# The first block of a convolution feeding a two-layer network: one part of the tokens convolved on TensorE, another in 256 columns, and the last sums made elsewhere

## The chip, the core and the metric

The kernel runs on one core of a Trainium2 chip (trn2). The metric is the device time of one execution in microseconds, as the median of several executions. A core has TensorE (PE, matrix multiplication; PEld is its weight load), VectorE (DVE), ScalarE (ACT), GpSimd (POOL) and SyncE (SP, here only the queue that issues most DMAs).

## The reference, cut to what matters

```python
# weight (8 heads, 7 taps); x (8, 4096, 192); w_in (192, 2048); w_out (2048, 192)
w = softmax(weight, axis=-1)
x_pad = concatenate([zeros((B, 6, D)), x], axis=1)
y[b, s, h, g] = sum over k of w[h, k] * x_pad[b, s + k, h, g]     # a causal filter of 7 taps
h = y.reshape(32768, 192) @ w_in
g = where(h >= 1, h, where(h <= -1, 0, (h + 1) ** 2 / 4))
out = g @ w_out
```

## The kernel before

**Tiles and steps.** The 32768 tokens are cut into 64 blocks of 512 (TB). The 2048 hidden units are cut into 8 pairs of 128. A step q is one block s and one pair j (q = 8 s + j). In step q TensorE does mm1(q), the first layer into the PSUM tile h, and then the second layer of step q - 2 (mm2, or mm2_first for the first two blocks). The tile h has two buffers (pool ps_h), so mm1(q + 2) waits until step q has read its h for the last time. That last read is most(q) in the first eight steps and act_max(q) later.

**Channels.** The 192 channels are 128 and 64. A pair of blocks c (tokens A and tokens B) is convolved in three units: "a" holds channels 0 to 127 of tokens A, "b" the same of tokens B, and "r" holds channels 128 to 191 of both, tokens A on partitions 0 to 63 (TOP) and tokens B on 64 to 127 (BOT). A unit is loaded (raw), transposed to channels on partitions (xT), and its seven taps are summed into y. Blocks from the second on need y split into a high and a low part (split, split_rest), and each part also with its two halves of partitions exchanged. The exchange is DMAs from SBUF to SBUF (swapped), two for each part, issued by SP.

**The first block** (s = 0, steps 0 to 7) has a program of its own. Its activation of step q is a ScalarE pass (Relu, then Square) and most(q) on VectorE. The weights arrive as 64-bit numbers in chunks 0 to 9 (words) and are turned into floats on the chip: ScalarE makes m and r (floats), VectorE makes wa in two instructions and adds r (bits), which gives WI (first layer, chunk j needed by mm1(j)) and WF (second layer). Chunk n's slot in words is free again when floats(n) is done, and chunk n + 3 is loaded into it.

**Convolution of the first two blocks before the change.** Unit a: taps 4, 5, 6 on VectorE, taps 0 to 3 and the join of the two on TensorE (taps_pe). Unit r: all seven taps on VectorE for both token blocks at once, then a TensorE copy of the upper half (both_pe). Only then do VectorE's bits of chunks 0 and 1 follow, and mm1(0). Unit b: taps on VectorE in steps 1 to 5 (FIRST_B), split in step 6. split_rest of unit r is in step 5. mm1(8) is the first matmul group of tokens B: it reads the high and low parts of b, of b exchanged, and of r.

**Order.** The order on every engine is the order in which the code is written (manual_schedule), and each engine works its list strictly in that order. Semaphores join the engines. DMAs of one queue are issued in order.

**The end** (evac_last): the last block's sums stand in two PSUM halves for each of accr (channels 128 up) and accm. ScalarE copies half 0 to SBUF; VectorE copies the first 256 columns of half 1 and adds the two halves in the other 256. TensorE transposes each block of 128 tokens, summing the halves as it does, and each of four results is copied and stored.

Of the kernel before, what the change touches and what calls it, by code (L numbers as in the profile page):

```python
# [8 lines left out]
F32 = mybir.dt.float32  # L9
# [21 lines left out]
def lightconv_then_ffn(ctx: ExitStack, tc: tile.TileContext, x, weight, w_in, w_out, out):  # L31
# [52 lines left out]
    def load_raw(t0s, chans, engs=None):  # L84


        raw = xin.tile([P, NG, SQ], F32, name="raw")
        first = [t0 % S == 0 for t0 in t0s]
        for i0 in (0, 2):
            if first[i0]:  # L90
                nc.gpsimd.memset(raw[i0 * SQ:(i0 + 2) * SQ, 0, :], 0.0)
        for i in range(4):
            lo = 1 if first[i] else 0
            src = xf[t0s[i] - SQ + lo * SQ:t0s[i] + TB, chans[i]:chans[i] + SQ]
            (engs[i] if engs else nc.sync).dma_start(
                out=raw[i * SQ:(i + 1) * SQ, lo:, :],
                in_=src.rearrange("(j a) b -> a j b", a=SQ),
            )
        return raw

    def load_plain(eng, c0, n, *t0s):

        raw = xin.tile([P, NG, SQ], F32, name="raw").rearrange("p j b -> p (j b)")[:, 0:TB]
        to = raw.rearrange("p (t i c) -> p t i c", t=TB // P, i=len(t0s))
        for i, t0 in enumerate(t0s):
            eng.dma_start(out=to[:, :, i], in_=xf[t0:t0 + TB, c0:c0 + n].rearrange(
                "(t p) c -> p t c", p=P))
        return raw

    def load_unit(c, u, engs=None):  # L110
        ta, tb = 2 * c * TB, (2 * c + 1) * TB
        if u == "r":
# [8 lines left out]
    class Conv:  # L121


        def __init__(self, c, u, raw):
            self.c, self.u, self.raw = c, u, raw
            self.wsel = 1 if u == "r" else 0

        def transpose(self):
            self.xT = xw.tile([P, NG * SQ], F32, name="xT")
            self.y = xw.tile([P, TB], F32, name="y")  # L130
            nc.vector.transpose(out=self.xT, in_=self.raw.rearrange("p j b -> p (j b)"))

        def transpose_pe(self, ps):

            self.ps = ps
            for t in range(0, TB, P):
                nc.tensor.transpose(ps[:, t:t + P], self.raw[:, t:t + P], one)  # L137

        def tail_pe(self, c0, ps):

            nc.tensor.matmul(ps, self.raw[:, c0:c0 + P], one[:, P - K + 1:], start=True, stop=True)

        def room(self):

            self.xT = xw.tile([P, NG * SQ], F32, name="xT")
            self.y = xw.tile([P, TB], F32, name="y")
            nc.vector.memset(self.xT[:, SH:SQ], 0.0)

        def fetch(self):
            nc.scalar.copy(self.xT[:, SQ:], self.ps)  # L150

        def taps_pe(self, banks, ks):

# [34 lines left out]
        def taps(self, *ks):  # L188
            y = self.y
            for k in ks:  # L190
                tap, wt = self.xT[:, SH + k:SH + k + TB], wk[:, self.wsel, k:k + 1]
                if k == 0:
                    nc.scalar.mul(y, tap, wt)
                else:
                    p = xw.tile([P, TB], F32, name="p", bufs=3)
                    nc.scalar.mul(p, tap, wt)  # L196
                    nc.gpsimd.tensor_add(y, y, p)  # L197
# [20 lines left out]
        def both_pe(self, bank):  # L218

            self.ys = [ps_o.tile([P, TB], F32, name=bank)]  # L220
            nc.tensor.matmul(self.ys[0], ident[TOP], self.y[TOP], start=True, stop=True)

        def split_rest(self):
# [253 lines left out]
    def evac_last(s):  # L477

# [5 lines left out]
        for a in "rm":  # L484
            u, v = part[a] = [ob.tile([P, TB], F32, name="t", bufs=4) for _ in range(2)]
# [4 lines left out]
        ps = [ps_h.tile([P, 2, TB], F32, name="h") for _ in range(2)]  # L490
        y = [ob.tile([P, TB], F32, name="sum") for _ in range(2)]
        for b in range(TB // P):
            i, e, n = b // 2, b % 2, slice(b * P, (b + 1) * P)
            for a, i_n, c in (("r", ident[:, 0:DR], slice(P, D)), ("m", plain, slice(0, P))):
                ts = part[a][i:]
                for t in ts:
                    nc.tensor.matmul(ps[e][:, i, c], t[:, n], i_n, start=(t is ts[0]),  # L497
                                     stop=(t is ts[-1]))
            to = y[i][:, e * D:(e + 1) * D]
            if e == 0:  # L500
                nc.scalar.copy(to, ps[e][:, i, 0:D])
# [33 lines left out]
    idle_matmuls(6)  # L535
    nc.scalar.dma_start(out=heads, in_=weight)
    raw_a = load_plain(nc.sync, 0, P, 0)
    raw_r = load_plain(nc.sync, P, DR, 0, TB)
    chunks[0].load(nc.sync)
    for n in range(1, 5):  # L540
        if n == 3:
            raw_b = load_unit(0, "b")
# [5 lines left out]
    for sel, c0, reps in ((0, 0, 1), (1, P, 2)):  # L548
# [22 lines left out]
    conv_a.fetch()  # L571
# [37 lines left out]
    whole(2, 0, CI)  # L609
    floats(2, CI)  # L610
# [8 lines left out]
    FIRST_B = {1: (0, 1), 2: (2,), 3: (3, 4), 4: (5,), 5: (6,)}  # L619
# [24 lines left out]
    for j in range(NPAIR):  # L644
        PARTS[5 + j].append((j, False))
# [127 lines left out]
```

## Time and profile before

| | us |
|---|---|
| median of 3 runs | 2262.39 (2261.7 to 2262.97) |
| the profiled execution | 2263.13 |
| its span, first to last instruction | 2261.3 |
| TensorE busy | 2253.2 |
| VectorE, ScalarE, GpSimd busy | 2110.2, 1694.2, 1160.5 |

The profiled execution is 0.74 us above the median. Of its 2263.13 us, 1.8 lie outside the span. All times in the tables below are counted from the span's first instruction.

### The profile page before, as it was taken

Reading aid. Unit: us, or ns where it says so; the run is one execution under the profiler, and the core shown is the slowest. Engines: PE = TensorE matmul, PEld = TensorE weight load, DVE = VectorE, ACT = ScalarE, POOL = GpSimd, SP = SyncE. Lnnn points to the kernel's source line nnn. Section 1 sums busy time; section 2 is a strip of 40 time slices with the busy share of each in tenths; the row PEclk is TensorE's granted clock in tenths of the full one; section 3 lists DMA queues with packets and bytes.
Section 4 is the critical chain, followed back from the end, with each engine's and each line's share of the span. In section 5 each row is a group of like instructions: output and inputs, shape, how many; then the busy total and the mean of one; then the engine's idle time right before and its main releaser. Section 6 shows DMA issues by size and latency. Waiting matters only on the chain.

```text
span 2261.3 us, 48195 instructions
## 1 busy us (share of the span) xinstructions
PE 2253.2 (100%) x19676; PEld 2096.3 (93%) x19676; DVE 2110.2 (93%) x1862; ACT 1694.2 (75%) x2141; POOL 1160.5 (51%) x846
## 2 busy tenths in 40 slices
PE   9999999999999999999999999999999999999999
PEld 6999999999999999999999999999999999999998
DVE  8899999999999999999999999999999999999997
ACT  6678777778777777777877777877777777787775
POOL 0446544466445565455654446644556545565451
PEclk9999999999999999999999999999999999999999
DMA  7221222222222222222122222222222222212211
GB/s 160 49 51 36 48 49 49 51 47 42 46 46 51 53 39 51 49 46 53 36 49 48 49 51 48 42 46 46 50 53 39 51 49 46 54 36 49 48 34 24
DMA packets 441852, 110.94 MB, mean 49 GB/s; under 512 B 410144, under 2 KB 417312, under 8 KB 441632
## 3 DMA queue, kind: packets, MB, share of 16 engines
q1 hardware_dynamic: 441472, 107.77, 25.8%
q8 instruction: 155, 2.54, 0.5%
q14 instruction: 65, 0.53, 0.1%
q10 hardware_dynamic: 160, 0.10, 0.0%
HBM read 32.83 MB, written 25.17 MB: 26 GB/s over the span
## 4 chain that ended last, share of the span: by engine, by line
PE 99%; DVE 0%; ACT 0%; issue 0%; POOL 0%; POOLq 0%; DVEq 0%
PE h L351 47%; PE accm L395 30%; PE accr L395 20%; PE accm L373 1%; PE accr L373 1%; DVE y L185 0%; PE h L497 0%; PE accm L529 0%; DVE g L679 0%; ACT g L669 0%; DVE y L183 0%; PE h L137 0%; PE accr L578 0%; DVE gh L311 0%; DVE wa L306 0%
## 5 line engine op out<-in xcount | busy, mean ns | idle before, releaser
L197 POOL TENSOR_TENSOR y<-y,p 128x512 f32<-128x512 f32 x558 | 779.9, 1398 | 794.2 <-DVE g L417 559.8
L430 DVE TENSOR_TENSOR gl<-g,gh 128x1024 fp32r<-128x1024 f32 (+1 forms) x497 | 734.0, 1477 | 27.2 <-ACT gh L424 22.7
L412 ACT ACTIVATE g<-g 128x1024 f32<-128x1024 f32 (+1 forms) x505 | 535.3, 1060 | 242.9 <-DVE g L406 234.2
L424 ACT CAST gh<-g 128x1024 fp32r<-128x1024 f32 (+1 forms) x497 | 521.6, 1050 | 239.4 <-DVE g L417 229.1
L406 DVE TENSOR_SCALAR g<-h 128x1024 f32<-128x1024 f32 (+1 forms) x505 | 610.0, 1208 | 94.7 <-PE h L351 86.4
L351 PE MATMUL h<-hi,w 64*128 64x512 f32 x4032 | 653.6, 389 | 0.0
L417 DVE TENSOR_TENSOR g<-h,g 128x1024 f32<-128x1024 f32 (+1 forms) x505 | 613.8, 1216 | 9.8 <-ACT g L412 2.4
L395 PE MATMUL accm<-gh,w 64*128 64x512 f32 x3968 | 548.1, 388 | 0.0
L351 PEld LDWEIGHTS h<-hi,w 64*128 64x128 f32 x4032 | 431.6, 184 | 29.1
L395 PEld LDWEIGHTS accm<-gh,w 64*128 64x128 f32 x3968 | 425.1, 184 | 28.9
L351 PE MATMUL h<-lo,w 64*128 64x512 f32 x2016 | 421.4, 388 | 0.0
L196 ACT ACTIVATE p<-xT,wk 128x512 f32<-128x512 f32 x558 | 372.1, 709 | 0.2 <-POOL y L197 0.2
L395 PE MATMUL accr<-gl,wr 64*128 64x512 f32 x1984 | 321.0, 388 | 0.0
L395 PE MATMUL accr<-gh,wr 64*128 64x512 f32 x1984 | 321.0, 388 | 0.0
L395 PE MATMUL accm<-gl,w 64*128 64x512 f32 x1984 | 321.0, 388 | 0.0
L351 PE MATMUL h<-rhi,w 64*128 64x512 f32 x1008 | 310.9, 388 | 0.0
L351 PE MATMUL h<-rh,w 64*128 64x512 f32 x1008 | 310.9, 388 | 0.0
L351 PEld LDWEIGHTS h<-lo,w 64*128 64x128 f32 x2016 | 216.0, 184 | 14.7
L443 POOL TENSOR_TENSOR sum<-t 128x512 f32<-128x512 f32 (+1 forms) x126 | 162.8, 1313 | 128.5 <-ACT t L442 128.5
L395 PEld LDWEIGHTS accr<-gl,wr 64*128 64x128 f32 x1984 | 212.6, 184 | 14.6 <-DVE gl L430 0.2
L395 PEld LDWEIGHTS accm<-gl,w 64*128 64x128 f32 x1984 | 212.6, 184 | 14.5
L395 PEld LDWEIGHTS accr<-gh,wr 64*128 64x128 f32 x1984 | 212.6, 184 | 14.5
(114 smaller groups left out, 1939.9 us busy)
## 6 DMA issues: line engine op xcount, KB each, us to landing
out_dram<-osb SPq DMA_DIRECT2D x366, 64.0 KB, 2.0
raw<-in_x_dram SPq DMA_DIRECT2D x334, 68.0 KB, 2.4
hi<-hi SPq DMA_DIRECT2D x126, 128.0 KB, 2.4
lo<-lo SPq DMA_DIRECT2D x126, 128.0 KB, 2.3
rhi<-rh SPq DMA_DIRECT2D x64, 128.0 KB, 2.3
rlo<-rl SPq DMA_DIRECT2D x64, 128.0 KB, 2.4
words<-in_moe_w_in_dram SPq DMA_DIRECT2D x16, 192.0 KB, 4.2
words<-in_moe_w_out_dram SPq DMA_DIRECT2D x8, 384.0 KB, 4.2
```

Source lines behind the costliest of these rows:

```text
L196: nc.scalar.mul(p, tap, wt)
L197: nc.gpsimd.tensor_add(y, y, p)
L351: nc.tensor.matmul(h[:, e, :], w[HALVES[e], COL[u][e]:COL[u][e] + P], x[e], start=(n == 0), stop=(n == len(mms) - 1))
L373: nc.tensor.matmul(accs[s][a, i][:, c0:c0 + D], g[half, e, b * P:(b + 1) * P], w[half, e, :], start=False, stop=(j == NPAIR - 1 and e == 1 ...
L395: nc.tensor.matmul(accs[s][a, i], st, g[HALVES[i], e, :], start=(j == 0 and n == first[a]), stop=(j == NPAIR - 1 and n == last[a]))
L406: nc.vector.tensor_scalar(out=g[:, e, :], in0=hs[q][:, e, :], scalar1=-1.0, scalar2=1.0, op0=ALU.max, op1=ALU.min)
L412: nc.scalar.activation(g[:, e, :], g[:, e, :], AF.Square, bias=0.5, scale=0.5)
L417: nc.vector.tensor_tensor(out=g[:, e, :], in0=h[:, e, :], in1=g[:, e, :], op=ALU.max)
L424: nc.scalar.copy(gh[:, e, :], gs[q][:, e, :])
L430: eng.tensor_sub(gl[:, e, :], g[:, e, :], gh[:, e, :])
L443: nc.gpsimd.tensor_add(y[:, n], t[0][:, n], t[1][:, n])
```

## The change

1. **Unit r of the first block** is loaded from tokens A alone, once as they are (partitions 0 to 63) and once one token later (64 to 127). One matmul over 128 rows with a diagonal of weights then applies two taps: pairs_pe does taps 1, 3, 5 and a single one for tap 6. It replaces seven taps on VectorE and both_pe.
2. **Unit a**: tap 0 on TensorE (tap_pe), taps 1 to 6 on VectorE, then join_pe. Its transposes and copies are in two halves, and the two spread matmuls stand between them. Five idle matmuls stand ahead instead of six, and the two in the middle are gone.
3. **Tokens B of channels 128 up** are a new unit "rb": 256 columns, the first half of tokens B on partitions 0 to 63 and the second on 64 to 127. Tap 0 is on ScalarE; taps 1 to 6 are a product on ScalarE and a sum on GpSimd, in steps 2 to 6. split_halves then needs three DMAs for each of two parts, from 256 columns each. Chunk 3, unit b, chunk 4 and rb are loaded after the floats of chunk 0 or 1.
4. **Unit b**: transposed in step 2, tap 0 on ScalarE there, taps 1 to 6 on VectorE in steps 3 to 6.
5. **Steps 0 and 1** have code of their own: chunks 2 and 3 are turned into floats in halves, and step 0's second half is clipped on VectorE. The splits of WI 0 and 1 (PARTS) move to steps 6 and 7. mm1 of the first block reads its operands in another order (ns, sn, rr).
6. **The end**: VectorE adds both halves of the columns, so TensorE does one matmul of each kind per block of tokens. The four results lie in four PSUM banks; the first two are stored with one DMA.

```diff
+        def tap_pe(self, banks, k):
+            self.ys = [ps_o.tile([P, TB], F32, name=i) for i in banks]
+            for half, y in zip(HALVES, self.ys):
+                nc.tensor.matmul(y, diag(self.u, k)[half], self.xT[half, SH + k:SH + k + TB],
+                                 start=True, stop=False)
+        def pairs_pe(self, bank, *ks):
...
+            for k in ks:
+                n = TOP if k == K - 1 else slice(0, P)
+                nc.tensor.matmul(self.ys[0], diag(self.u, k)[n], self.xT[n, SH + k:SH + k + TB],
+                                 start=(k == 1), stop=(k == K - 1))
...
+        def split_halves(self):
...
+            for key, t in (("hi", hi), ("lo", lo)):
+                w = xo.tile([P, TB], F32R, name="r" + key, bufs=2)
+                t32, w32 = t.bitcast(F32), w.bitcast(F32)
+                for to, half in ((t32[TOP, late], BOT), (w32[BOT, late], BOT),
+                                 (w32[BOT, 0:n], TOP)):
+                    nc.sync.dma_start(out=to, in_=t32[half, 0:n])
...
     def evac_last(s):
...
-            nc.vector.tensor_copy(out=v[:, half], in_=acc[a, 1][:, half])
-            nc.vector.tensor_tensor(out=v[:, rest], in0=acc[a, 1][:, rest], in1=u[:, rest],
-                                    op=ALU.add)
+            for n in (half, rest):
+                nc.vector.tensor_tensor(out=v[:, n], in0=acc[a, 1][:, n], in1=u[:, n], op=ALU.add)
...
-    conv_a.taps_dve(4, 5, 6, first=4)
-    conv_a.taps_pe(("accm0", "accm1"), range(4))
-    conv_r.fetch()
-    nc.vector.tensor_copy(out=conv_r.xT[BOT, SH:SQ], in_=tail_r[BOT, 0:K - 1])
-    conv_r.taps_dve(*range(K))
+    conv_a.taps_dve(*range(1, K), first=1)
+    conv_a.tap_pe(("accm0", "accm1"), 0)
+    conv_r.pairs_pe("accr0", 1, 3, 5)
+    conv_a.join_pe()
+    conv_r.pairs_pe("accr0", K - 1)
     floats(0)
...
-    FIRST_B = {1: (0, 1), 2: (2,), 3: (3, 4), 4: (5,), 5: (6,)}
+    FIRST_B = {3: (1, 2), 4: (3,), 5: (4, 5), 6: (6,)}
+    FIRST_RB = {2: (0, 1), 3: (2,), 4: (3,), 5: (4,), 6: (5, 6)}
...
     def first_step(q):
...
+        a, f, b = both_square(q, g), chunks[n].floats(), chunks[n].bits()
+        advance(a, f, a)
+        if q < 6:
+            advance(b)
+        else:
+            conv_b.taps_dve(*FIRST_B.get(q, ()))
+        most(q, g)
+        hs.pop(q)
+        conv_rb.taps(*FIRST_RB.get(q, ()))
+        if q == 6:
+            conv_b.split(nc.vector)
+        advance(f)
+        if q < 6:
+            advance(b)
+            if q == 2:
+                conv_b.transpose()
+                conv_b.taps(0)
+            conv_b.taps_dve(*FIRST_B.get(q, ()))
+        if q == 6:
+            conv_rb.split_halves()
```

**Three places in the engines' lists.** On VectorE, at the top of the program, this stood between the weights of the taps (wk) and the first finished piece of w_in (gh is the tile that holds it); y sums taps of xT:

```order
L183 TENSOR_SCALAR y<-xT,wk 128x512 [waits DVE_49,Activation_49]
L185 SCALAR_TENSOR_TENSOR y<-xT,wk,y 128x512 [waits DVE_49] x2
L599 COPY xT<-h 64x6 [waits PE_49]
L183 TENSOR_SCALAR y<-xT,wk 128x512 [waits DVE_49,Activation_49]
L185 SCALAR_TENSOR_TENSOR y<-xT,wk,y 128x512 [waits DVE_49] x6
L304 TENSOR_SCALAR wa<-m 128x384 [waits Activation_49]
L306 SCALAR_TENSOR_TENSOR wa<-m,wa 128x384 [waits DVE_49]
L311 ISA gh<-wa,r 128x768 [waits DVE_49,Activation_49]
```

The same place of the change, on VectorE:

```order
L199 TENSOR_SCALAR y<-xT,wk 128x512 [waits DVE_49,Activation_49]
L201 SCALAR_TENSOR_TENSOR y<-xT,wk,y 128x512 [waits DVE_49] x5
L332 TENSOR_SCALAR wa<-m 128x384 [waits Activation_49]
L334 SCALAR_TENSOR_TENSOR wa<-m,wa 128x384 [waits DVE_49]
L339 ISA gh<-wa,r 128x768 [waits DVE_49,Activation_49]
```

Ten instructions on y or xT became six.

On ScalarE, steps 2 and 3 of the change: two taps of rb (y and p with 256 columns) and tap 0 of unit b (512 columns) stand ahead of the Relu of step 3, and tap 0 waits for VectorE's transpose of unit b.

```order
L711 ACTIVATE g<-h 128x1024 [waits PE_49]
L320 ACTIVATE m<-words 128x768 [waits DMAHW4_49,DMAHW5_49,DMAHW3_49,DVE_49]
L713 ACTIVATE g<-g 128x1024 [waits Activation_49]
L210 ACTIVATE y<-xT,wk 128x256 [waits DVE_49]
L213 ACTIVATE p<-xT,wk 128x256
L322 ACTIVATE r<-words 128x768
L210 ACTIVATE y<-xT,wk 128x512 [waits DVE_49]
L711 ACTIVATE g<-h 128x1024 [waits PE_49]
L320 ACTIVATE m<-words 128x768 [waits DMAHW4_49,DMAHW3_49,DMAHW2_49]
```

Before, ScalarE had no tap in these steps, only the Relu, Square, m and r.

On SP, the exchanges that mm1(8) waits for, before (rh, rl are the parts of r, hi, lo those of b):

```order
L202 DMA rhi<-rh 64x512 [waits DMAHW4_49,Activation_49]
L203 DMA rhi<-rh 64x512 [waits DMAHW5_49]
L202 DMA rlo<-rl 64x512 [waits DMAHW6_49,DVE_49]
L203 DMA rlo<-rl 64x512 [waits DMAHW7_49]
L202 DMA hi_563<-hi_559 64x512 [waits DMAHW0_49,Activation_49]
L203 DMA hi_563<-hi_559 64x512 [waits DMAHW1_49]
L202 DMA lo_566<-lo_560 64x512 [waits DMAHW2_49,DVE_49]
L203 DMA lo_566<-lo_560 64x512 [waits DMAHW3_49]
```

and in the change:

```order
L219 DMA hi_574<-hi_570 64x512 [waits DMAHW1_49,Activation_49]
L220 DMA hi_574<-hi_570 64x512 [waits DMAHW2_49]
L219 DMA lo_577<-lo_571 64x512 [waits DMAHW3_49,DVE_49]
L220 DMA lo_577<-lo_571 64x512 [waits DMAHW4_49]
L260 DMA rh<-rh 64x256 [waits DMAHW5_49,Activation_49]
L260 DMA rhi<-rh 64x256 [waits DMAHW6_49]
L260 DMA rhi<-rh 64x256 [waits DMAHW7_49]
L260 DMA rl<-rl 64x256 [waits DMAHW0_49,DVE_49]
L260 DMA rlo<-rl 64x256 [waits DMAHW1_49]
L260 DMA rlo<-rl 64x256 [waits DMAHW2_49]
```

Those of the channels from 128 went from ahead of unit b's to behind them, and from four to six.

## Rows read from the trace of the kernel before

**Rows 1.** The page, its first part: busy time of each engine.

```profile
PE 2253.2 (100%) x19676; PEld 2096.3 (93%) x19676; DVE 2110.2 (93%) x1862; ACT 1694.2 (75%) x2141; POOL 1160.5 (51%) x846
```

**Rows 2.** Timeline of TensorE, 0 to 60: start, length, instructions, [idle before, releaser].

```profile
13.80 1.12 PE L221 MATMUL accr<-y,ident 64*128 64x512 f32 x2 [2.37 <-DVE y L185]
15.46 3.56 PE L351 MATMUL h<-hi,gh 64*128 64x512 f32 x8 [0.54 <-DVE gh L311]
...
23.11 1.99 PE L351 MATMUL h<-hi,gh 64*128 64x512 f32 x8 [0.53 <-DVE g L679]
...
28.68 1.91 PE L351 MATMUL h<-hi,gh 64*128 64x512 f32 x8
...
31.26 0.84 PE L373 MATMUL accm<-wf,g 64*128 64x192 f32 x8
...
56.64 0.84 PE L373 MATMUL accm<-wf,g 64*128 64x192 f32 x8
```

**Rows 3.** Stretches of 2 us: length, busy by engine, granted TensorE clock, DMA.

```profile
16.00:18.00 2.00, 2.00 (x8) 0.92 (x6) 1.72 (x4) 1.33 (x4) 0.00 (x0) 0.50 1.10 231
```

**Rows 4.** Timeline of VectorE, 0 to 60.

```profile
9.06 4.69 DVE L185 SCALAR_TENSOR_TENSOR y<-xT,wk,y 128x512 f32<-128x512 f32 x6
...
17.18 0.36 DVE L304 TENSOR_SCALAR wa<-m 128x384 uint32<-128x384 uint32 x1
...
18.93 0.36 DVE L304 TENSOR_SCALAR wa<-m 128x384 uint32<-128x384 uint32 x1
...
25.00 0.74 DVE L131 STREAM_TRANSPOSE xT<-raw 128x544 f32<-128x544 f32 x1
...
27.70 0.56 DVE L304 TENSOR_SCALAR wa<-m 128x768 uint32<-128x768 uint32 x1
...
29.17 0.49 DVE L183 TENSOR_SCALAR y<-xT,wk 128x512 f32<-128x512 f32 x1
...
30.36 0.55 DVE L311 CUSTOM_DVE_ANT_0 gl<-wa,r 128x768 uint16<-128x768 uint16 x1
...
31.30 1.21 DVE L679 SCALAR_TENSOR_TENSOR g<-g,h 128x1024 f32<-128x1024 f32 x1
32.43 0.55 DVE L304 TENSOR_SCALAR wa<-m 128x768 uint32<-128x768 uint32 x1
```

**Rows 5.** Timeline of ScalarE, 0 to 60.

```profile
5.14 0.59 ACT L150 COPY xT<-h 128x512 f32<-128x512 f32 x1 [2.10 <-PE h L137]
...
31.49 1.02 ACT L669 ACTIVATE g<-h 128x1024 f32<-128x1024 f32 x1 [1.57 <-PE h L351]
...
34.16 0.93 ACT L292 ACTIVATE m<-words 128x768 f32<-128x768 f32 x1
...
48.51 0.62 ACT L211 CAST hi<-y 128x512 fp32r<-128x512 f32 x1 [0.46 <-DVE y L185]
```

**Rows 6.** Timeline of SP's queue, 46 to 52.

```profile
49.16 0.46 SPq L202 DMA_DIRECT2D hi<-hi  x1
...
50.95 0.59 SPq L203 DMA_DIRECT2D lo<-lo  x1
```

**Rows 7.** DMA issues, 45 to 52: count, KB each, median us from issue to landing.

```profile
lo<-lo SPq DMA_DIRECT2D x2, 128.0 KB, 2.3
```

**Rows 8.** Lines L332 and L197, all instructions: ns min/median/max, first and last start.

```profile
L332 DVE TENSOR_TENSOR wr<-wf,wr x8: 281/1372/1378, 63.0 to 96.1; 128x128 fp32r<-128x128 f32 x8
...
L197 POOL TENSOR_TENSOR y<-y,p x558: 1270/1300/2808, 61.4 to 2203.2; 128x512 f32<-128x512 f32 x186
```

**Rows 9.** The page, costliest groups: busy us, mean ns of one, idle before.

```profile
L417 DVE TENSOR_TENSOR g<-h,g 128x1024 f32<-128x1024 f32 (+1 forms) x505 | 613.8, 1216 | 9.8 <-ACT g L412 2.4
```

**Rows 10.** Timelines of TensorE and VectorE at the end, 2225 to 2262.

```profile
2256.09 0.56 PE L497 MATMUL h<-ident,t 128*128 128x64 f32 x4
...
2255.46 0.42 DVE L488 TENSOR_TENSOR t<-accm,t 128x256 f32<-128x256 f32 x1
...
2258.35 0.36 DVE L503 COPY sum<-h 128x192 f32<-128x192 f32 x1 [0.80 <-PE h L497]
```

More of the change, by code (lines that the diff above doesn't have):

```diff
@@ L130, in transpose @@
             self.y = xw.tile([P, TB], F32, name="y")
[L131 to L141, printed above, removed]
+            n = self.n + SQ
+            nc.vector.transpose(out=self.xT[:, 0:n],
+                                in_=self.raw.rearrange("p j b -> p (j b)")[:, 0:n])
@@ L195, in taps @@
                     p = xw.tile([P, TB], F32, name="p", bufs=3)
[L196 to L197 removed]
+                    nc.scalar.mul(p[:, 0:n], tap, wt)
+                    nc.gpsimd.tensor_add(y, y, p[:, 0:n])
         def swapped(self, t, name, bufs):
@@ L534, in lightconv_then_ffn @@
     nc.vector.memset(warm, 0.0)
-    idle_matmuls(6)
+    idle_matmuls(5)
     nc.scalar.dma_start(out=heads, in_=weight)
[L537 to L542, printed above, removed]
+    raw_a = load_plain(nc.sync, 0, P)
+    raw_r = load_plain(nc.sync, P, DR, late=True)
+    for n in range(3):
         chunks[n].load(nc.sync)
@@ L654, in parts_lo, with advance, both_square, most @@
             chunks[n].lo(rest)
-    bits = {LAG: chunks[LAG].bits(CI)}
-    next(bits[LAG])
+    def advance(*steps):
+        for i in steps:
+            next(i)
+    def both_square(q, g):
+        h = hs[q]
+        nc.scalar.activation(g, h, AF.Relu, bias=0.5, scale=0.5)
+        yield
+        nc.scalar.activation(g, g, AF.Square)
+        yield
+    def most(q, g, e=slice(0, 2)):
+        h = hs[q]
+        nc.vector.scalar_tensor_tensor(out=g[:, e], in0=g[:, e], scalar=1.0, in1=h[:, e],
+                                       op0=ALU.min, op1=ALU.max)
@@ new lines, in lightconv_then_ffn, with step_0 @@
+    pre = {(n, c): (chunks[n].floats(*cs), chunks[n].bits(*cs))
+           for n, c, cs in ((2, "i", (0, CI)), (2, "o", (CI,)), (3, "i", (0, CI)), (3, "o", (CI,)))}
+    def step_0():
+        h = hs[0]
+        g = g32[0] = act.tile([P, 2, TB], F32, name="g", bufs=3)
+        (_, b2), (f2o, b2o), (f3, _) = pre[2, "i"], pre[2, "o"], pre[3, "i"]
+        advance(f2o, b2)
+        nc.scalar.activation(g[:, 0], h[:, 0], AF.Relu, bias=0.5, scale=0.5)
+        nc.vector.tensor_scalar(out=g[:, 1], in0=h[:, 1], scalar1=-1.0, scalar2=1.0,
+                                op0=ALU.max, op1=ALU.min)
+        nc.scalar.activation(g[:, 1], g[:, 1], AF.Square, bias=0.5, scale=0.5)
+        advance(b2)
+        nc.scalar.activation(g[:, 0], g[:, 0], AF.Square)
+        nc.vector.tensor_tensor(out=g[:, 1], in0=h[:, 1], in1=g[:, 1], op=ALU.max)
+        most(0, g, slice(0, 1))
+        hs.pop(0)
+        advance(f2o, f3)
+        advance(b2o, b2o)
@@ L659, in first_step, with step_1 @@
+    def step_1():
+        g = g32[1] = act.tile([P, 2, TB], F32, name="g", bufs=3)
+        (f3, b3), (f3o, b3o) = pre[3, "i"], pre[3, "o"]
+        chunks[5].load(nc.sync)
+        a = both_square(1, g)
+        advance(a, f3, a, b3, b3)
+        most(1, g)
+        hs.pop(1)
+        advance(f3o, f3o, b3o, b3o)
+        conv_rb.transpose()
     def first_step(q):
-        n = q + LAG + 1
+        n = q + LAG
         if n + 2 < NCH:
             chunks[n + 2].load(nc.sync)
-        h = hs.pop(q)
@@ L686, in first_step @@
-        if q > 0:
-            most()
-        if n < NCH:
-            words[n] = chunks[n].floats()
-            next(words[n])
-            bits[n] = chunks[n].bits()
-            next(bits[n])
+        advance(f)
[7 more added lines that the diff above has]
+            conv_rb.split_halves()
         parts_hi(q + 1)
         parts_lo(q)
-        if q == 0:
-            conv_b.transpose()
```

192 lines of the change are left out of this document (104 added, 88 removed).

## The prediction

> **What bounds the kernel now.** The page comes first: TensorE is busy for 2253.2 of 2261.3 us [rows 1]. So I look for the places where it waits or runs slowly. TensorE's timeline shows three waits in the whole execution, all in the first 24 us [rows 2]: 2.37 us for the last tap of unit r on VectorE, 0.54 us for the first finished weights, 0.53 us for most(0). [...] The eight instructions at 15.46 take 3.56 us; the same eight at 28.68 take 1.91 [rows 2]. So a fall of the clock costs 1.65 us here. From 23.11 on TensorE never waits until the end. The change therefore can win only ahead of 23.11 and behind the last matmul, and what it wins in front it keeps only if steps 2 to 8 still cause no wait.
>
> **The start, won.** VectorE did three taps of a and seven of r; now it does six taps of a. The first can start when the second half of unit a is copied, by my estimate at about 6.15. (A whole copy ended at 5.73 [rows 5]; the two halves come after the spread matmuls.) Six taps are one of 0.52 and five of 0.78 (4.69 for six [rows 4]), so they end at 10.6; before, the last tap ended at 9.06 + 4.69 = 13.75. From there to mm1(0) it was 15.46 - 13.75 = 1.71, so mm1(0) starts at 12.3. Unit r's three pair matmuls are hidden ahead of the join, in time in which TensorE would wait for the taps. The trace has no matmul of 128 rows by 512 columns; L221, with 64 rows, took 1.12 [rows 2], so I take 0.9 each and 1.1 as the upper bound. Only the fourth, for tap 6, lies between join and mm1(0), where VectorE's conversion of chunk 0 covers it to within 0.2.
>
> TensorE now waits 0.7 there instead of 2.37, so I expect the upper clock level. mm1(0) and mm1(1) take 2.58 each (28.68 to 31.26 [rows 2]) and end at 14.9 and 17.5. Then mm1(2) needs h(0). Clip, Square and two VectorE passes, each of 512 columns, are four links of about 0.7 (1024 columns take 1.21 [rows 4]), which gives 17.8. mm1(2) starts at 17.9 instead of 23.11: **5.2 us won**.
>
> **Steps 2 to 8, given back.** From 23.11 to the second layer of step 8 at 56.64 are 33.53 us without a wait [rows 2]. If nothing new waited, that point would now be at 51.4. But mm1(8) needs unit b and rb split and exchanged, and these sit at the end of a chain on VectorE:
>
> - From 17.8: three half chunks at 1.75 (17.18 to 18.93), most(1) 1.13 (31.30 to 32.43), the transpose of rb (nothing to 0.74; 0.40 by its 288 of 544 columns), one step without taps, the transpose of b 0.74 [rows 4]. A step with two taps was 27.70 to 32.43 = 4.73, its taps 29.17 to 30.36 = 1.19, so without taps it is 3.54 [rows 4]. Sum 11.06: unit b is transposed at 28.9.
> - ScalarE's tap 0 of b waits for that transpose, and behind it in the queue stand Relu of step 3 (whose matmuls are done at about 26) and m of chunk 5. These are 0.59, 1.02 and 0.93 [rows 5], less 0.1 of overlap each: m is there at 31.3. VectorE has stood still for 2.4 us.
> - Then steps 3, 4 and 5 (3 x 3.54) and the six taps of b (6 x 0.78) are 15.3: tap 6 ends at 46.65.
> - ScalarE's cast of b takes 0.62 [rows 5], to 47.3. SP then issues ten exchanges in a row. The last four of before are (50.95 - 49.16) / 3 = 0.60 apart [rows 6]; six of the new ones are half as large, and the shortest issue took 0.46, so I take 0.55 between bounds of 0.46 and 0.60. The tenth is issued at 52.25 and lands 2.3 later [rows 7], at 54.55. The last two matmuls of mm1(8) need it, so the second layer of step 8 starts at 54.8. That is 1.85 earlier than 56.64, not 5.2.
>
> **GpSimd in the way.** Before, GpSimd's first add came at 61.4; now it adds six products of 256 columns in steps 2 to 6. An add of 512 columns took 1.27 at least. While one ran, VectorE's wr (two operands in SBUF) took 1372 ns instead of 281 [rows 8]: it lost 1.09, 0.86 of the add. L417, which reads PSUM and SBUF, shows no loss: its mean is 1216 [rows 9], like most with 1.21 when GpSimd was idle [rows 4]. By my times the adds of taps 1 and 2 fall beside most(2) and most(3), and cost nothing. Those of taps 3, 4, 5 and 6 fall between instructions that read SBUF alone. An add of 256 columns is about half of 1.27, 0.64, so each costs VectorE 0 to 0.64; by wr's share 0.55, and I take that. Four are 2.2, all on the chain to tap 6: the second layer of step 8 starts at 57.0, **0.35 later than before**.
>
> [...]
>
> **Hidden edits.** The three DMAs for r, and the loads that move behind the floats of chunks 0 and 1, are hidden if they land before 17 us (chunk 3), 22 (chunk 4), 23.5 (rb) and 28 (b); uncovered, each us late is a us on the chain. Moving the splits of WI 0 and 1 costs nothing, since mm1(8) waits longer for the exchanges.
>
> **The end.** The last add of the two halves ended at 2255.46 + 0.42 = 2255.88, and the last copy at 2258.35 + 0.36 = 2258.71 [rows 10]. Now the first half's add has to wait for ScalarE, so the last add is 0.35 later, at 2256.25. Behind it stand two transposes and what is left of the four passes ahead of them, at 0.14 each (four in 0.56 [rows 10]), about 0.45, the 0.3 that a result takes to arrive, and one copy of 0.36: 2257.45. That is **1.2 us earlier**, between 0.8 and 1.4. The store behind it is of the same kind.
>
> **The sum.** 2263.13 + 0.35 - 1.2 = 2262.3 for the profiled execution. That was 0.74 above the median, so I forecast a median of 2261.5.
>
> **The rivals.**
> - *The clock falls (slower than before).* While TensorE waits for the exchanges it stands for some 4 of 6 us in several pieces. Before, 2.37 and 0.54 of 4 us went ahead of the fall [rows 2]. If it falls as the waits end, mm1(8) and the next matmuls cost 1.65 more: 2263.1. This decides the sign, because the forecast gains only 0.9. Against it: matmuls stand between the pieces, and a fall during the wait costs less.
> - *GpSimd costs nothing.* Its adds fall beside passes that read PSUM, or VectorE's taps do not block as wr did. Then 1.85 + 1.2 remain: 2259.3.
> - *The exchanges do not hold mm1(8).* If tap 0 does not hold ScalarE, VectorE saves its 2.4 us, and if the issues are also shorter, TensorE keeps nearly all of 5.2 + 1.2: 2256.0. For it: before, exchanges were never waited for. Against it: ten now follow one cast, where four did.
> - *Later still.* A late load of rb, or the clock and the whole 0.64 together: 2264 and more.
>
> **Chances.** Forecast 0.36; clock 0.26; no cost by GpSimd 0.19; no wait for exchanges 0.11; later still 0.08. The range leaves out the last two: 2257.8 to 2264.0, where the lower end is the case without GpSimd's cost (2259.3) with issues at 0.46 (0.8 less), the transpose of rb at nothing (0.4) and an end of 1.4 (0.2), and the upper end the clock's case with the whole 0.64 and issues at 0.60. About 0.2% (4.5 us) is what a measurement of this kernel can tell from no change. Faster by more than that is the case without a wait for exchanges and a bit beside it, 0.12; slower by more takes several mishaps, 0.03; within it 0.85.
>
> **What would show it.** mm1(0) near 12.3 and mm1(2) near 17.9 at the upper clock; on ScalarE a wait of more than 2 us at tap 0 of b; wa or taps on VectorE lengthened by some 0.55 four times; tap 6 near 48.8; TensorE waiting for DMAs in mm1(8), the second layer of step 8 near 57; a last copy 1.2 earlier behind the last matmul. The prediction is wrong if mm1(8) does not wait for rh and rl, or if VectorE's chain is already late at 17.8.

## The result: 5.1 us slower, by the trace of the change

The change takes 2266.86 us at its median (15 executions, 2265.73 to 2267.32), the kernel before 2261.74 beside it (2261.65 to 2263.3): ratio 1.0020, 95% interval 1.0012 to 1.0028. The forecast was 2261.5, the range ended at 2264.0. The forecast gave a chance of 0.03 to being slower by more than 4.5 us. Executions of either kernel differ by some 1.6 us; the profiles below show TensorE's clock low at other moments in each (granted 0.50 from 57.6 to 64.4 us in the change, from 15.7 to 19.2 in the kernel before), so what follows compares rows, and medians only for the total.

The profiled execution took 2267.32. Its steps beside those of the prediction:

| step | predicted | profile of the change |
|---|---|---|
| mm1(0) starts | 12.3 | 14.27 |
| mm1(2) starts | 17.9 | 20.51 |
| tap 6 of b ends | 48.8 | 49.83 |
| SP's exchanges, one from the next | 0.55 | 0.63 |
| second layer of step 8 | 57.0 | 58.38 |
| lower clock behind it | none | 57.6 to 64.4 |
| TensorE's wait for unit a's taps | 0.7 | none |
| last copy behind the last matmul | 1.2 earlier | 1.26 earlier |
| total | 2262.3 | 2267.32 |

TensorE's timeline of the change, the start and then steps 8 to 10. The first four rows answer to the start in [rows 2]; mm1(8) starts at 52.48, mm1(9) at 63.41 and mm1(10) at 68.54:

```profile
6.42 1.28 PE L148 MATMUL h<-sum,raw 128*128 128x128 f32 x4 [0.18 <-DMA raw<-in_x_dram]
7.63 2.08 PE L163 MATMUL accm<-xT,t 64*128 64x512 f32 x4
9.64 2.90 PE L178 MATMUL accr<-xT,t 128*128 128x512 f32 x6
12.47 1.13 PE L169 MATMUL accm<-y,ident 64*128 64x512 f32 x4
...
14.27 1.98 PE L381 MATMUL h<-hi,gh 64*128 64x512 f32 x8
...
20.51 1.99 PE L381 MATMUL h<-hi,gh 64*128 64x512 f32 x8 [0.83 <-DVE g L719]
...
52.48 0.52 PE L381 MATMUL h<-hi,w 64*128 64x512 f32 x1
...
56.41 0.47 PE L381 MATMUL h<-rhi,w 64*128 64x512 f32 x1 [0.80 <-DMA rhi<-rh]
...
58.38 0.76 PE L381 MATMUL h<-rlo,w 64*128 64x512 f32 x1 [0.92 <-DMA rlo<-rl]
58.38 1.72 PE L403 MATMUL accm<-wf,g 64*128 64x192 f32 x7
...
63.41 0.88 PE L381 MATMUL h<-hi,w 64*128 64x512 f32 x1
...
68.54 0.53 PE L381 MATMUL h<-hi,w 64*128 64x512 f32 x1
```

The same places of the kernel before:

```profile
54.43 0.53 PE L351 MATMUL h<-hi,w 64*128 64x512 f32 x1
...
59.11 0.53 PE L351 MATMUL h<-hi,w 64*128 64x512 f32 x1
```

mm1(8) waits for the exchanges, as forecast: it takes from 52.48 to 58.38, 5.90 instead of 2.21 (54.43 to 56.64). But the second layer behind it takes from 58.38 to 63.41, 5.03 instead of 2.47 (56.64 to 59.11). Its first eight instructions took 0.84 in [rows 2]; here seven take 1.72. Stretches of 2 us of the same execution (the column behind the five engines is the granted clock; compare [rows 3]):

```profile
54.00:56.00 2.00, 1.46 (x4) 0.55 (x3) 1.59 (x2) 1.22 (x3) 0.00 (x0) 1.00 0.54 120
56.00:58.00 2.00, 1.04 (x4) 0.48 (x4) 1.83 (x5) 0.00 (x0) 0.00 (x0) 0.89 0.44 98
58.00:60.00 2.00, 1.62 (x10) 1.65 (x12) 1.60 (x3) 0.00 (x0) 0.00 (x0) 0.50 0.04 8
...
62.00:64.00 2.00, 2.00 (x16) 2.00 (x14) 1.41 (x2) 2.00 (x4) 0.28 (x1) 0.50 0.00 0
64.00:66.00 2.00, 2.00 (x18) 1.83 (x17) 0.00 (x0) 0.25 (x1) 1.92 (x2) 0.90 0.00 0
```

TensorE is busy for 1.46 and 1.04 of 2 us, then the granted clock is 0.50 from 57.6 to 64.4, with full work from 58.38 on, for 6 us. VectorE's timeline of the change; the first row is taps 2 to 6 of unit a, the others answer to [rows 4]:

```profile
7.20 3.90 DVE L201 SCALAR_TENSOR_TENSOR y<-xT,wk,y 128x512 f32<-128x512 f32 x5
...
17.79 0.69 DVE L732 TENSOR_SCALAR g<-h 128x512 f32<-128x512 f32 x1 [1.16 <-ACT g L731]
...
33.50 0.56 DVE L332 TENSOR_SCALAR wa<-m 128x768 uint32<-128x768 uint32 x1 [2.50 <-ACT m L320]
...
39.08 1.36 DVE L334 SCALAR_TENSOR_TENSOR wa<-m,wa 128x768 uint32<-128x768 uint32 x1
...
43.10 1.09 DVE L332 TENSOR_SCALAR wa<-m 128x768 uint32<-128x768 uint32 x1
...
47.16 2.67 DVE L201 SCALAR_TENSOR_TENSOR y<-xT,wk,y 128x512 f32<-128x512 f32 x3
```

and ScalarE's, where tap 0 of b holds up what stands behind it:

```profile
31.04 0.72 ACT L210 ACTIVATE y<-xT,wk 128x512 f32<-128x512 f32 x1 [2.43 <-DVE xT L141]
31.67 1.00 ACT L711 ACTIVATE g<-h 128x1024 f32<-128x1024 f32 x1
32.57 0.90 ACT L320 ACTIVATE m<-words 128x768 f32<-128x768 f32 x1
```

The end, from the last matmul of the sums (compare [rows 10]):

```profile
2259.39 0.40 PE L425 MATMUL accm<-gl,w 64*128 64x512 f32 x2
...
2262.06 0.36 DVE L529 COPY sum<-accr 128x192 f32<-128x192 f32 x1 [0.26 <-PE accr L527]
```

and the last matmul of the sums in the kernel before:

```profile
2254.42 0.40 PE L395 MATMUL accm<-gl,w 64*128 64x512 f32 x2
```

From that matmul's end to the last copy's end are 2.63 us (2259.79 to 2262.42) where it was 3.89 (2254.82 to 2258.71).

### The profile page after: what moved, and what is told of

The parts are those of the page before. It is cut to its first block, busy times and chain, and to the rows that moved or that the text cites. A ratio compares the mean times of both kernels' runs of the same rounds, so it can differ in the third digit from the quotient of the medians.

```text
span 2265.6 us, 48183 instructions
## 1 busy us (share of the span) xinstructions
PE 2256.8 (100%) x19653; PEld 1928.7 (85%) x19653; DVE 2107.6 (93%) x1861; ACT 1697.5 (75%) x2155; POOL 1168.1 (52%) x852
## 4 chain that ended last, share of the span: by engine, by line
PE 98%; DVE 1%; issue 0%; ACT 0%; DMA 0%; SPq 0%; DVEq 0%
PE h L381 46%; PE accm L425 30%; PE accr L425 20%; PE accr L403 1%; PE accm L403 1%; DMA raw<-in_x_dram 0%; PE accr L178 0%; ACT g L711 0%; DVE y L201 0%; SPq L260 0%; DMA rlo<-rl 0%; PE accm L163 0%; DVE wa L332 0%; ACT m L320 0%; DVE gl L339 0%
## 5 line engine op out<-in xcount | busy, mean ns | idle before, releaser
L214 POOL TENSOR_TENSOR y<-y,p 128x512 f32<-128x512 f32 (+1 forms) x564 | 787.2, 1396 | 790.5 <-DVE g L447 560.4
L381 PE MATMUL h<-hi,w 64*128 64x512 f32 x4032 | 780.3, 389 | 0.0
L425 PE MATMUL accm<-gh,w 64*128 64x512 f32 x3968 | 652.6, 388 | 0.0
L381 PE MATMUL h<-lo,w 64*128 64x512 f32 x2016 | 633.9, 388 | 0.2 <-DMA lo<-lo 0.2
L381 PEld LDWEIGHTS h<-hi,w 64*128 64x128 f32 x4032 | 570.0, 185 | 64.6 <-DMA hi<-hi 0.2
L425 PE MATMUL accr<-gh,wr 64*128 64x512 f32 x1984 | 425.7, 388 | 0.0
L425 PE MATMUL accr<-gl,wr 64*128 64x512 f32 x1984 | 425.6, 388 | 0.0
L425 PE MATMUL accm<-gl,w 64*128 64x512 f32 x1984 | 425.5, 388 | 0.0
L381 PEld LDWEIGHTS h<-lo,w 64*128 64x128 f32 x2016 | 371.6, 184 | 33.1 <-DMA lo<-lo 0.8
L213 ACT ACTIVATE p<-xT,wk 128x512 f32<-128x512 f32 (+1 forms) x564 | 375.1, 707 | 0.2 <-POOL y L214 0.2
```

The costliest lines, as they stand in the source:

```text
L213: nc.scalar.mul(p[:, 0:n], tap, wt)
L214: nc.gpsimd.tensor_add(y, y, p[:, 0:n])
L381: nc.tensor.matmul(h[:, e, :], w[HALVES[e], c0:c0 + P], x[e][e], start=(n == 0), stop=(n == len(mms) - 1))
L425: nc.tensor.matmul(accs[s][a, i], st, g[HALVES[i], e, :], start=(j == 0 and n == first[a]), stop=(j == NPAIR - 1 and n == last[a]))
```

## The experiments

Four theories at first: the start is late because of TensorE's clock (or because unit r's data come late); the exchanges hold mm1(8) because of VectorE's chain; the stretch behind is slow because TensorE stood still; the end gives what was forecast. Twelve kernels, each as an edit of the change unless another is named, all timed against the kernel before.

**The end alone** (the kernel before with the new evac_last).

> The kernel before with the change's end alone. By the prediction's term the last copy comes 1.2 us earlier behind the last matmul of the sums, and the median falls by the same, to about 2260.5. By the trace of the change the last copy is 1.25 earlier but the last store takes longer, and the span ends only 0.7 earlier: about 2261.0. Rival: the end gives nothing, 2261.7.

2261.03 against 2262.30, ratio 0.9995 (0.9986 to 1.0004): not told apart. Its shortest execution is 2260.90, that of before 2261.65, so 0.75. Its start is that of the kernel before, and its profile shows something else:

```profile
14.05 1.12 PE L221 MATMUL accr<-y,ident 64*128 64x512 f32 x2 [0.16 <-DVE y L185]
15.71 1.99 PE L351 MATMUL h<-hi,gh 64*128 64x512 f32 x8 [0.54 <-DVE gh L311]
...
21.66 1.99 PE L351 MATMUL h<-hi,gh 64*128 64x512 f32 x8 [0.53 <-DVE g L681]
```

The same eight matmuls at the start of mm1(0) took 3.56 in [rows 2], and mm1(2) came at 23.11. So the profiled execution of before had met a fall of the clock (granted 0.50 in 16 to 18 us [rows 3]) that this one, by its 1.99, did not: TensorE had stood for 2.37 ahead of L221 there, and for 0.16 here. The 15 executions of before lie in two groups, 2261.65 to 2261.74 and 2262.39 to 2263.3; that the upper one is the one with the fall is likely, and not shown.

**Eight idle matmuls.**

```diff
-    idle_matmuls(5)
+    idle_matmuls(6)
...
+    idle_matmuls(2)
     conv_r.transpose_pe(xT_0[:, 1], *range(TB // P))
```

> The change with the eight idle matmuls of the kernel before (six at the start instead of five, two ahead of unit r's transposes). Theory: the start is late because TensorE's clock rises only at 9.8 us instead of 5.5, so that the transposes, the two matmuls of tap 0 and the first pair run at the lower level; with the idle matmuls the clock rises near 5.5, mm1(0) starts at about 12.6 instead of 14.27, the exchanges follow 1.7 earlier, and the time is about 2265.2 (the wait in mm1(8) and the slow stretch behind it stay). Rival: unit r's late load (its third DMA takes 2.01 us to issue) sets the start: mm1(0) stays near 14 and the time at 2266.9.

2266.82, ratio 1.0018 (1.0009 to 1.0027): no gain at the median, where the theory had 2265.2 and the rival 2266.9. In its profile:

```profile
6.78 0.30 PE L148 MATMUL h<-sum,raw 128*128 128x128 f32 x1 [0.53 <-DMA raw<-in_x_dram]
7.26 0.55 PE L148 MATMUL h<-sum,raw 128*128 128x128 f32 x3 [0.18 <-DMA raw<-in_x_dram]
7.75 1.13 PE L163 MATMUL accm<-xT,t 64*128 64x512 f32 x4
8.80 2.84 PE L178 MATMUL accr<-xT,t 128*128 128x512 f32 x6
...
13.38 1.98 PE L381 MATMUL h<-hi,gh 64*128 64x512 f32 x8
```

L163 takes 1.13 instead of 2.08, and mm1(0) comes 0.9 earlier (at 13.38, not at the expected 12.6); r's late data (0.71 of waiting) take part of what else was to be won. Both theories hold a part.

**Unit rb one step earlier.**

```diff
-    FIRST_RB = {2: (0, 1), 3: (2,), 4: (3,), 5: (4,), 6: (5, 6)}
+    FIRST_RB = {2: (0, 1), 3: (2,), 4: (3, 4), 5: (5, 6)}
...
-        if q == 6:
+        if q == 5:
             conv_rb.split_halves()
```

> The change with tap 4 of rb in step 4, taps 5 and 6 in step 5, and rb's split with its six exchanges at the end of step 5 instead of step 6, so that only the four exchanges of b stand behind the cast of b. Theory: mm1(8) then waits for lo only, the second layer of step 8 starts at about 55.6 instead of 58.4, the clock stays at the upper level, and 2.8 + 2.9 us come back: about 2261.3. Rival one: the clock falls all the same behind the shorter wait: about 2264. Rival two: VectorE's chain to tap 6 of b is the limit and becomes later by the added work in step 5: 2265 or more.

2263.25, ratio 1.0002 (0.9993 to 1.0011): 3.6 of the 5.1 come back. In its profile mm1(8) waits only for lo (0.17), and by the lengths the clock stays up: seven of L403 behind it take 0.88, where they took 1.72 in the change. The 2 us that are missing to the expected 2261.3 lie partly in step 10, which takes 5.70 (63.01 to 68.71) where it takes 5.02 before and in the change (taken up below).

**Matmuls with weights of zero in the wait.**

```diff
+            for _ in range({5: 3, 6: 3, 8: 4}.get(n, 0) if q == NPAIR else 0):
+                nc.tensor.matmul(h[:, 0, :], nought[:, 0:P], busy.bitcast(BF16)[:, 0:TB],
+                                 start=False, stop=False)
```

> The change with ten matmuls with weights of zero in mm1(8) (three ahead of the last two on s, three ahead of the first on r, four ahead of the last two on r), each 128 rows by 512 columns of bf16, added to h. They add nothing to the sums and stand where TensorE waits for exchanges anyway. [...] Rival: the slow stretch of 6 us behind the wait is not caused by TensorE standing idle (or zeros do not count as work): 2266.9 or a little more.

2264.80, ratio 1.0010 (1.0001 to 1.0019). The author's estimate was 2264.0, the change's 2266.86 without the 2.9 us of the slow stretch; the rival had 2266.9. Timeline and stretches of its profile; L380 are the zero matmuls:

```profile
57.05 1.04 PE L380 MATMUL h<-osb 128*128 128x512 bf16 x4
...
58.38 0.46 PE L384 MATMUL h<-rlo,w 64*128 64x512 f32 x1
58.38 0.95 PE L406 MATMUL accm<-wf,g 64*128 64x192 f32 x7
...
65.63 0.52 PE L384 MATMUL h<-hi,w 64*128 64x512 f32 x1
```

```profile
58.00:60.00 2.00, 2.00 (x22) 1.83 (x23) 1.87 (x3) 0.00 (x0) 0.00 (x0) 1.00 0.00 0
```

mm1(0) starts at 14.26 and the last matmul of mm1(8) at 58.38, as in the change, and step 10 at 65.63 instead of 68.54. So the clock's fall costs 2.9 us between these two profiles, and it stays away with the zero matmuls in the waits: the granted clock is 1.00 in every stretch from 54 to 66. The medians are 2.1 apart; the profiled execution of the change is its slowest.

**Tap 0 of b in step 3.**

```diff
         advance(a, f, a)
+        if q == 3:
+            conv_b.taps(0)
...
             if q == 2:
                 conv_b.transpose()
-                conv_b.taps(0)
```

> The change with tap 0 of unit b on ScalarE moved from step 2 into step 3, behind Relu, m and Square of step 3, so that ScalarE no longer stands waiting for the transpose of b ahead of them. Theory: VectorE's idle 2.50 us ahead of chunk 5 goes nearly away, tap 6 of b ends at about 47.8 instead of 49.83, TensorE no longer waits for gl in steps 5 and 6 (0.5 in all), the tenth exchange lands 2 us earlier, the second layer of step 8 starts at about 56.4, and the time is about 2264.9, with the slow clock behind it as before. Rival: ScalarE is only moved from one wait to another and m of chunk 5 comes no earlier: tap 6 within 0.5 of 49.8, time 2266.9.

2262.87, ratio 1.0001 (0.9992 to 1.0010): 4.0 of 5.1 from one moved instruction. VectorE in its profile:

```profile
31.10 0.74 DVE L141 STREAM_TRANSPOSE xT<-raw 128x544 f32<-128x544 f32 x1
31.76 0.52 DVE L332 TENSOR_SCALAR wa<-m 128x768 uint32<-128x768 uint32 x1
...
41.95 0.56 DVE L332 TENSOR_SCALAR wa<-m 128x768 uint32<-128x768 uint32 x1 [0.88 <-ACT m L320]
...
45.49 2.32 DVE L201 SCALAR_TENSOR_TENSOR y<-xT,wk,y 128x512 f32<-128x512 f32 x3
```

mm1(2) started at 21.34, so from there to the end of tap 6 (47.81) are 26.47 instead of 29.32. Of these 2.85 ScalarE's wait at tap 0 is 2.50; the adds now fall where they lengthen nothing (1.29 more), and a wait of 0.88 is new. mm1(8) still waits (0.31 and 0.92) and takes 4.19, but the granted clock stays at 1.00 in this profile (every stretch from 52 to 62); that, besides the shorter chain, is why it gained twice what was expected.

**Without GpSimd's adds.**

```diff
-                    nc.gpsimd.tensor_add(y, y, p[:, 0:n])
+                    if self.u != "rb":
+                        nc.gpsimd.tensor_add(y, y, p[:, 0:n])
```

> The change without GpSimd's six additions for unit rb: its products are made, but y stays that of tap 0, so the channels from 128 of the second block of tokens are left without taps 1 to 6. It prices the adds. By the prediction they cost VectorE 2.2 us ahead of tap 6 (2264.7); by the trace of the change three of VectorE's instructions are longer by 0.40, 0.54 and 0.34, so 1.3 (tap 6 at 48.5, second layer of step 8 at 57.1, time 2265.6); by the rival in which GpSimd costs nothing 2266.9.

2264.73, ratio 1.0009 (1.0000 to 1.0019). The median meets the prediction's figure, but the rows do not. VectorE:

```profile
34.61 0.56 DVE L333 TENSOR_SCALAR wa<-m 128x768 uint32<-128x768 uint32 x1 [2.49 <-ACT m L321]
...
47.32 2.32 DVE L201 SCALAR_TENSOR_TENSOR y<-xT,wk,y 128x512 f32<-128x512 f32 x3
```

From mm1(2) at 21.62 to the end of tap 6 at 49.64 are 28.02: the adds cost 1.30, not 2.2. Three of VectorE's rows had been longer in the change, by 0.40, 0.53 and 0.35. The rest of the gain is the clock, which stayed at 1.00 in this profile (every stretch from 54 to 64). Its last two waits are as long as in the change (0.80 and 0.91), but mm1(8) as a whole takes 4.82 instead of 5.90:

```profile
53.37 0.53 PE L382 MATMUL h<-hi,w 64*128 64x512 f32 x1
...
58.19 0.46 PE L382 MATMUL h<-rlo,w 64*128 64x512 f32 x1 [0.91 <-DMA rlo<-rl]
```

```profile
56.00:58.00 2.00, 1.05 (x4) 0.48 (x4) 1.83 (x5) 0.00 (x0) 0.00 (x0) 1.00 0.43 96
58.00:60.00 2.00, 1.81 (x22) 1.84 (x24) 1.92 (x3) 0.05 (x1) 0.00 (x0) 1.00 0.03 8
```

**Unit r's shifted copy loaded by ScalarE.**

```diff
...
-            eng.dma_start(out=to[:, 1:, 1],
+            late.dma_start(out=to[:, 1:, 1],
...
```

> The change with the two DMAs of unit r's shifted copy issued by ScalarE instead of SP. Theory one (unit r's load makes the start late): SP has its 2.0 us for the words of chunks 0 to 2, unit r's transposes no longer wait, mm1(0) starts at about 13.6 instead of 14.27, time 2266.2. Theory two (the low clock up to 9.8 makes it late): mm1(0) stays at 14.1 or later, 2266.9. Rival: the issue takes 2 us on ScalarE as well and holds the Exp of the tap weights there: mm1(0) at 15, 2267.7.

2270.09, ratio 1.0033 (1.0021 to 1.0046): the rival's mechanism, and more than its 2267.7. On ScalarE:

```profile
1.71 1.76 ACTq L111 DMA_DIRECT2D raw<-in_x_dram  x1
3.50 1.28 ACT L579 ACT_TABLE_LOAD   x1 [3.50 <-issue]
```

The issue is nearly as long there, Exp is behind it, and the tap weights are 2.1 late. Unit r came later, too: in this profile TensorE waits 1.21 for it, and mm1(0) starts at 18.26 instead of the expected 15. It leaves open what an earlier r would give.

**Three edits together**: rb earlier, tap 0 in step 3, and step 0 through ScalarE, in place of the clip and the max on VectorE:

```diff
...
+        for e in range(2):
+            nc.scalar.activation(g[:, e], h[:, e], AF.Relu, bias=0.5, scale=0.5)
...
+        for e in range(2):
+            most(0, g, slice(e, e + 1))
```

> Three edits of the change together: rb's taps and split one step earlier (as the run with rb earlier), tap 0 of b in step 3, and step 0's activation as in the kernel before (both halves through ScalarE, no clip on VectorE). Theory: mm1(2) 0.3 earlier, no wait for gl, the last of four exchanges of b lands at about 52.7, ahead of its matmuls, so that TensorE keeps its lead to step 8: second layer of step 8 at about 53.7, time about 2259.5, faster than both kernels. Rival: the lead is given back behind step 8, where the second layer of step 8 waits for ScalarE's copies of the first block's sums, late behind the new taps: 2261.5.

2261.24, ratio 0.9994 (0.9986 to 1.0003): near the rival's 2261.5, not the theory's 2259.5. TensorE's wait for most(0) is 0.45 instead of 0.83, mm1(8) waits for nothing. Its profile shows the rest:

```profile
9.76 4.35 PE L178 MATMUL accr<-xT,t 128*128 128x512 f32 x6
...
15.85 1.98 PE L381 MATMUL h<-hi,gh 64*128 64x512 f32 x8
...
65.11 0.70 PE L397 MATMUL accr<-osb 64*128 64x384 bf16 x2
...
68.06 0.53 PE L381 MATMUL h<-hi,w 64*128 64x512 f32 x1
```

The pairs take 4.35 where they took 2.84 with eight idle matmuls, and mm1(0) comes at 15.85. Step 10 takes 5.65 (62.41 to 68.06): two of L397, which clears the banks of the first block's sums for the next block, take 0.70 on accr there, where two took 0.33 at 24.55. That ScalarE's copies of these sums hold them is the rival's reading, and no row shows it.

**The clock alone** (eight idle matmuls and the zero matmuls).

> The change with the eight idle matmuls of the kernel before and with the ten matmuls of weight zero in mm1(8), and nothing moved: TensorE's clock alone. Theory: the clock rises near 5 us (4.5 in the run with eight idle matmuls, 9.8 to 12.8 in seven profiles of kernels with five), mm1(0) starts at about 13.4, and it does not fall behind the exchanges: 0.9 less than the run with the zero matmuls, about 2263.9. Rival: when the clock rises differs from execution to execution and does not hang on the idle matmuls: the same as with the zero matmuls alone, 2264.8.

2264.53, ratio 1.0010 (1.0001 to 1.0019); mm1(0) at 12.96 in its profile, but the median only 0.3 below that of the zero matmuls alone, between the theory and the rival.

**Three edits and eight idle matmuls.**

> The run with three edits (2261.2 at its median, mm1(0) at 15.85 in its profile) with the eight idle matmuls of the kernel before as well. Theory: the clock rises near 5 us, mm1(0) starts at about 13.4, the exchanges follow, and the median is about 2259.5. Rival: the rise is not tied to the idle matmuls, and the median stays at 2261.2; or the start's lead is given back at mm1(8), which then waits for the exchanges: 2260.5 or more.

2260.40, ratio 0.9990 (0.9982 to 0.9999); mm1(0) at 14.14 in its profile, and mm1(8) waits for nothing. The 0.8 below the three edits alone is half of what the theory had.

**Three edits and the splits of WI 0 and 1 where they were.**

```diff
-        PARTS[5 + j if j > 1 else 6 + j].append((j, False))
+        PARTS[5 + j].append((j, False))
```

> The run with three edits with the splits of WI 0 and 1 in steps 5 and 6 again instead of 6 and 7. There VectorE has two splits in step 7, its clip of step 8 starts 2.1 us after the matmuls are done, ScalarE's Square of step 9 and the copies of the first block's sums are late behind it, and step 10 takes 5.65 us where it takes 5.01 in the kernel before. Theory: VectorE is 0.47 earlier in step 7, step 10 takes about 5.2, time 2260.8. Rival: the clip is held by the words of the last chunk and the transposes of the next unit, not by the split, and nothing changes: 2261.2; or the split in step 5 makes the chain to the exchanges 0.5 later and mm1(8) waits: 2261.5.

2260.69, ratio 0.9992 (0.9983 to 1.0001). With the splits there step 10 takes 5.19 in the profile of all five, below (60.83 to 66.02), about the 5.2 that was expected. So moving the splits is not free once mm1(8) no longer waits.

**All five.**

> All five edits together (rb one step earlier, tap 0 of b in step 3, step 0 through ScalarE, the splits of WI 0 and 1 in steps 5 and 6, eight idle matmuls). Theory: both gains add up, median about 2259.1, faster than the kernel before by 3 us (ratio 0.9987). Rival: mm1(8) waits for the exchanges when the start is earlier: 2260.5.

2259.89, ratio 0.9987 (0.9978 to 0.9996): faster than the kernel before (the theory had 2259.1), and 7.0 below the change's median. In its profile mm1(8) waits for nothing.

The start in all profiles that share it (durations of the rows of L163 and L178, in us):

| kernel | idle | 4 of L163 | 6 of L178 | mm1(0) |
|---|---|---|---|---|
| clock alone | 8 | 1.13 | 2.85 | 12.96 |
| eight idle | 8 | 1.13 | 2.84 | 13.38 |
| three + idle | 8 | 1.46 | 2.84 | 14.14 |
| all five | 8 | 1.59 | 2.84 | 14.27 |
| three + splits | 5 | 2.08 | 3.21 | 14.07 |
| zero matmuls | 5 | 2.08 | 3.31 | 14.26 |
| the change | 5 | 2.08 | 2.90 | 14.27 |
| rb earlier | 5 | 2.08 | 3.35 | 14.31 |
| tap 0 later | 5 | 2.08 | 4.04 | 15.10 |
| no adds | 5 | 2.08 | 3.96 | 15.37 |
| three | 5 | 2.08 | 4.35 | 15.85 |
| r by ScalarE | 5 | 2.08 | 3.98 | 18.26 |

The granted clock is listed as 1.00 where it was read (the change up to 24 us, eight idle matmuls from 3 to 7), so the level is read here from the lengths alone: 2.08 against 1.13 is a ratio of 1.8, like the 3.56 of L351 at a granted clock of 0.50 [rows 2, rows 3] against 1.99 of the same eight. By that reading L163 ran at the lower level in every profile with five idle matmuls, and in part or not at all with eight. By it, too, when the clock rises differs between executions of the same start (2.90 to 4.35 for the pairs with five), which may be why the medians show less than the rows: 0.0 and 0.3 in the change and with the zero matmuls, 0.8 in the two others.

## Why the prediction was wrong

The forecast case came in its mechanism: ScalarE held by tap 0 (2.43 measured, 2.4 worked out), ten exchanges behind one cast, mm1(8) waiting. The step that decided against it is the clock behind that wait, which the sum put at nothing. By its own sign, VectorE's chain already late at 17.8, it was wrong as well (mm1(2) at 20.51). What failed, by its own steps:

- **"TensorE now waits 0.7 there ..., so I expect the upper clock level"** in the start. TensorE did not wait: unit a's taps ended at 11.10 and the join began at 12.47, right behind the three pair matmuls, which were to be hidden ahead of it. mm1(0) came 1.97 late; 0.5 of it are the taps, 1.4 the pairs. By their lengths the transposes and tap 0 ran at the lower level (four of L163 took 2.08, and 1.13 with eight idle matmuls), and the two idle matmuls in the middle were gone. The step read a clock from one wait, and asked only whether it would fall, not when it rises. The clock is not all of it: with eight idle matmuls and L163 at 1.13, too, the join (11.58) waited for the pairs and not for the taps.
- **"Four links"** of step 0: there are five. The clip on VectorE follows ScalarE's Relu of the other half instead of running beside it (17.79, idle 1.16 behind ACT g), and adds to mm1(2)'s lateness, 2.61 in all. Why it does is open.
- **The adds** at 2.2: 1.30 measured. The sign and the place were right; they fell partly beside work that they do not lengthen. With the chain from mm1(2) to tap 6 shorter by 1.6 than worked out (the adds are 0.9 of it), 1.0 of the 2.6 was left at tap 6, and nine longer issues (0.63 for 0.55, 0.7 in all), less a landing of 2.0 instead of 2.3, made it 1.4 at step 8. That the second layer of step 8 came so near is in part luck: two errors cancel.
- **The clock's fall as a rival only, at 1.65.** It came in the profile, and cost 2.9, since some 6 us of full work ran at it, and not one group of eight matmuls as in [rows 2]. This is the largest term; at 2.9 instead of 1.65 the rival itself would have been 2264.4, above the range. The forecast had already placed some 4 us of standing there, and mm1(8) did take 3.7 more than before; "matmuls stand between the pieces" did not keep the clock up. In the change's profile the granted clock is 0.50 from the wait for rl on (57.6 to 64.4), and the zero matmuls price it at 2.9.
- **The end**: the last copy was right (1.26), though the terms listed for it add up to 2257.36 and not 2257.45, and no run shows the 0.3 that a result takes to arrive by itself: from the last add to the last copy's start are 0.87 (2261.19 to 2262.06), where the terms give 0.75, and from the last matmul's end in the profile (2262.03) to that start 0.03. But the span ended 5.8 us behind the last matmul of the sums (2265.6 - 2259.79), where it was 6.5 (2261.3 - 2254.82): 0.7 and not 1.2. From the last copy to the span's end were 2.6 and are 3.2, so "of the same kind" did not hold for the last store. The run of the end alone gives 0.75.

"Moving the splits of WI 0 and 1 costs nothing" did hold: step 10 took 5.02 in the change (68.54 to 73.56) as before (63.79 to 68.81). It costs 0.46 there (5.65 - 5.19) only in the kernels whose mm1(8) no longer waits.

The sum: 2262.3 + 1.4 (step 8) + 2.9 (clock) + 0.5 (end) = 2267.1; the profile has 2267.32. The base was off as well: it took 0.74 between the profiled execution and the median for a constant. The profile of before held a fall of the clock; against the profile with the end alone, which has none by its lengths (1.99 for the eight that took 3.56), mm1(2) is 23.11 - 21.66 = 1.45 later. So of the "5.2 won" only 3.8 could be won against an execution without it.

What stays open: in which executions the clock falls. In the profiles of the change, with eight idle matmuls and with r loaded by ScalarE mm1(8) took 5.90, 5.90 and 5.91 and the clock fell (seven of L403 behind it took 1.72, 1.72 and 1.48); without the adds, with tap 0 later and with rb earlier it took 4.82, 4.19 and 3.36, and the clock stayed up (the same seven took 0.95, 0.95 and 0.88). With one profile of each, it is not shown whether it falls in every execution of the former and in none of the latter. Open is also what an earlier load of unit r would give.

## What to carry to other kernels

Price a wait of TensorE as its length plus what the clock may take behind it (2.9 here), and look for the stretch of lower clock in the profile of before first: if one is there, that execution's time is not the base of the sum. In a queue worked in order, ask of each moved instruction what stands behind it while it waits: tap 0 on ScalarE, worth 0.7 us itself, decided 4.0 of the 5.1. A kernel that is let through one wait early may be held at the next place (step 10 here, 5.65 where it took 5.02), so follow it one step past the wait that is removed. And do not take it for granted that an engine waits where it waited before: TensorE's wait for the taps, in which the pairs were to be hidden, was gone.

## What was not expected of the hardware

With matmuls whose weights are zero in the waits, the granted clock stayed at 1.00 from 54 to 66 us, where it was 0.50 from 57.6 to 64.4 without them (2.9 us). One DMA's issue held SP for 2.01 us and ScalarE for 1.76, where the DMAs ahead of it on SP take 0.4 to 0.5. ScalarE's product of 256 columns takes 0.51 where 512 take 0.72, so halving the columns saves under a third.
